# When eight DRAM to DRAM additions of a two-layer block are put into the DMA queue: two moved up, two moved behind a product

## The chip, the cores and the metric

The kernel runs on one core of one Trainium2 chip. The metric is the time of one launch on the device, in microseconds (us), as the median of several runs.

The engines are named as in the profile: PE multiplies matrices, ACT copies, casts and applies functions, DVE adds and subtracts, POOL and SP issue DMA transfers (POOL the adding ones, SP plain ones). Each engine takes its instructions in the order of the program and waits on semaphores.

## The reference

Attention with a sigmoid, a gated block, and a second block on the Fourier transform of the result. The change lies in the last product of the last block:

```python
X = np.fft.fft(x, axis=1)
X = np.fft.fft(X, axis=2)
mixed = np.real(X).astype(np.float32)
u = x + mixed
...
un = (u - mu) / np.sqrt(var + 1e-06)
ch = np.maximum(un @ w_ch1, 0.0) @ w_ch2
return (u + ch).astype(np.float32)
```

There are four batch rows of 448 tokens, 768 features, and 3072 hidden features. All is float32.

## The kernel before, in words

Batch rows 0 and 1 go through both products directly. Batch rows 2 and 3 go through them together, by a scheme with seven block products in the place of eight. The hidden features are taken in twelve groups `g` of 256. A first product (`pair1`, PE tiles `f_X`, `f_Y`, `f_Z`, `f_W`) makes two groups, and then a *pass* `p` of the second product (`second`, PE tiles `m_...`) takes these two groups. There are five passes, p = 0 to 4 (`NS` is 5); the last two groups go through the plain product at the end (PE `f<-extra,v_h` and `f<-h,v_h`), whose pieces DVE adds to `acc`.

One pass has seven products, k = 0 to 6, and each product has three pieces, e = 0 to 2. A piece is six matmuls of 128x448. PE leaves a piece in one of five PSUM banks (`bank2`), ACT copies it into one of six slots of the tile `stage` (`second_done`, line 1204), and POOL adds the slot to a sum in DRAM by a DMA with `accum_op=add` (line 244), or to two sums. So a slot is free again when its additions have landed, and a bank when ACT has copied it. A piece that ACT can't copy for want of a slot holds the bank; five pieces later PE waits.

The sums in DRAM are `u_d[2]` and `u_d[3]` (six tiles each, one for each 128 features; `first(b)` is tiles 0 to 2, `last(b)` tiles 3 to 5) and four helpers `m_d[0]` to `m_d[3]` of three tiles each. Which product goes where is written in `second_done`. In the passes before the last, products 0 to 3 go to `m_d[0]` to `m_d[3]`, product 4 to `first(2)`, product 5 to `last(2)`, product 6 to `first(3)`. In the last pass product 0 goes to `m_d[3]` and `first(2)` at once, product 1 to `last(3)` and `first(3)` at once: two additions for each piece.

The generator `combine` adds the helpers into the sums where they belong, by DMAs from DRAM to DRAM of 672 KB (or 448 and 224 KB): `m_d[0]` into `m_d[3]` and `first(2)`, `m_d[1]` into `last(3)` and `first(3)`, `m_d[3]` into `m_d[2]` and `first(3)`, and at the end `m_d[2]` into `last(2)` and `last(3)`. Then it loads `u_d[2]` and `u_d[3]` into `acc`, in four loads on SP, for the additions of the plain product.

The order of instructions comes from a clock of the planner (`Order`): each generator yields the planned time at which it wants to go on, `need` waits for a key's planned time, and what a generator calls is put on its engine's queue at that point. On the chip the order of each queue is then fixed, and the waits are semaphores. Two DMAs on the same bytes wait for each other's landing, and a DMA that waits holds up all that stands behind it on POOL.

In the program's rows `u_d_141` is `u_d[2]`, `u_d_142` is `u_d[3]`, and `m_d_219` to `m_d_222` are `m_d[0]` to `m_d[3]`.

Of the kernel before, what the change touches and what calls it, by code (L numbers as in the profile page):

```python
# [111 lines left out]
NS = NG // 2 - 1  # L112
# [140 lines left out]
def build(tc, ap):  # L253
    nc = tc.nc
    V, G = nc.vector, nc.gpsimd
    o = Order(nc)
# [945 lines left out]
    def second_done(p, k, e, ps):  # L1202
        st = m_t["stage"][:, (3 * (7 * p + k) + e) % KD]
        yield o.act(st, ps)
        if k > 3:
            outs = [u_d[2 + k // 6][:, e + 3 * (k == 5)]]
        elif p < NS - 1 or k > 1:
            outs = [m_d[k][:, e]]
        elif k == 0:
            outs = [m_d[3][:, e], u_d[2][:, e]]  # L1210
        else:
            outs = [u_d[3][:, e + 3], u_d[3][:, e]]
        t = max([o.dma(out, st, add=p > 0 or k > 3) for out in outs])
        o.at["sum", k, e, p] = t + 6.0
        yield o.now

    def combine():

        def first(b):
            return u_d[b][:, 0:3]  # L1220

        def last(b):
            return u_d[b][:, 3:6]

        def landed(*ks, p=NS - 1):
            yield from o.need(*(("sum", k, e, p) for k in ks for e in range(3)))

        yield from landed(0, 3, p=NS - 2)
        for c in (slice(0, 2), slice(2, 3)):
            o.dma(m_d[3][:, c], m_d[0][:, c], add=True)  # L1230
        yield o.now + 8.0
        o.dma(first(2), m_d[0], add=True)
        yield from landed(6, p=NS - 2)
        o.dma(last(3), m_d[1], add=True)
        yield o.now + 8.0
        o.dma(first(3), m_d[1], add=True)
        yield from landed(0, 2, 3)
        for c in (slice(0, 2), slice(2, 3)):
            o.dma(m_d[2][:, c], m_d[3][:, c], add=True)
        o.dma(first(3), m_d[3], add=True)  # L1240
        yield o.now + 10.0
        o.dma(last(2), m_d[2], add=True)
        o.dma(last(3), m_d[2], add=True)
        yield from o.need(("hs", 7 * NS - 1))
        acc[2] = np_.tile([128, KD, S], F32, tag="x2", name="acc2", bufs=3)
        t = o.dma(acc[2][:, 0:3], first(2)) + 4.0
        o.at.update((("accs", 2, e), t) for e in range(3))
        yield from landed(5)
        t = o.dma(acc[2][:, 3:6], last(2)) + 4.0
        o.at.update((("accs", 2, e), t) for e in range(3, 6))  # L1250
        yield from landed(6)
        acc[3] = np_.tile([128, KD, S], F32, tag="x2", name="acc3", bufs=3)
        for x, src, es in ((acc[3][:, 0:3], first(3), range(3)), (acc[3][:, 3:6], last(3), range(3, 6))):
            t = o.dma(x, src) + 4.0
            o.at.update((("accs", 3, e), t) for e in es)
        yield o.now
# [71 lines left out]
    def network():  # L1328
# [88 lines left out]
        def second(p, ks):  # L1417
            for k in ks:
                m = 7 * p + k
                yield from o.need(("sw", m), ("hs", m))  # L1420
                (wh, wl), hs = sw_t[m], hs_t[m]
                for e in range(3):
                    es = slice(128 * e, 128 * e + 128)

                    def pair(i, wh=wh, wl=wl, hs=hs, es=es):
                        return wh[:, i, es], wl[:, i, es], hs[i][:, 0], hs[i][:, 1]

                    mark = ("part", m, e)
                    yield from o.tile(partial(bank2, f"m_{m}_{e}"), 2, pair, partial(second_done, p, k, e), mark)
                while len(o.feed) > 6:  # L1430
                    yield o.now + 0.1
            while ("part", m, 2, 1) not in o.at:
                yield o.now + 0.1
# [57 lines left out]
    o.spawn(late_rows())  # L1491
    o.spawn(second_rows())
    o.spawn(combine())
    o.spawn(second_weights())
    o.spawn(second_weights2())
# [64 lines left out]
```

## Time and profile before

| | |
|---|---|
| median of three runs | 1195.19 us (1195.03 to 1195.59) |
| time of the profiled execution | 1194.45 us |
| its span | 1192.7 us |
| PE busy | 1175.1 us, 99% of the span |
| DVE, ACT, POOL busy | 890.8, 575.0, 101.7 us |
| bytes in HBM | 149.35 MB read, 103.86 MB written |

The span is that of the engines' instructions, and the time of the execution has 1.75 us around it. A busy PE is one with a matmul in it, at whatever clock: the granted clock of TensorE is 1 at 2.4 GHz and 0.5 at 1.2 GHz.

### The profile page before, as it was taken

To read this page: it belongs to the slowest core of one execution; us is meant where nothing else is said; L and a number is where in the kernel's file an instruction comes from. 1 tells how busy PE (TensorE), PEld (TensorE's weight loads), DVE (VectorE), ACT (ScalarE), POOL (GpSimd) and SP (SyncE) were. 2 spreads that over 40 slices of the span, in tenths; PEclk is the share of its full clock that TensorE was granted. 3 is DMA by queue.
4 is the path that set the end of the run, shared out by engine and by line. 5 is a ranking of instruction groups with operands and counts; after the bars stand their busy time and mean duration, and the time that the engine had idled before them with its cause. 6 is when DMAs were issued, how large, how long until landed. Compare 5 with 4: busy or idle time off the path is not lost.

```text
span 1192.7 us, 16593 instructions
## 1 busy us (share of the span) xinstructions
PE 1175.1 (99%) x6040; PEld 1028.7 (86%) x6040; DVE 890.8 (75%) x1442; ACT 575.0 (48%) x1054; POOL 101.7 (9%) x142
## 2 busy tenths in 40 slices
PE   8999999999999999999999999999999999999798
PEld 3477767789999999999999999999999999999698
DVE  5686897656853669797999989899577777777472
ACT  5877777757540122242333333333247667665440
POOL 0000000000000000000000000000000234243530
PEclk9999999999999999999999999999999999999899
DMA  6757679766948556386556555645917598889996
GB/s 221 223 177 243 238 233 351 250 237 231 321 170 257 194 166 220 101 311 236 184 195 212 205 205 190 240 173 186 348 65 221 92 189 133 172 177 194 206 169 208
DMA packets 95009, 248.79 MB, mean 209 GB/s; under 512 B 11280, under 2 KB 48208, under 8 KB 94544
## 3 DMA queue, kind: packets, MB, share of 16 engines
q1 hardware_dynamic: 78416, 216.90, 52.5%
q0 software_dynamic: 16368, 30.62, 15.7%
q8 instruction: 47, 0.77, 0.3%
q14 instruction: 34, 0.28, 0.1%
q10 hardware_dynamic: 144, 0.23, 0.1%
HBM read 149.35 MB, written 103.86 MB: 212 GB/s over the span
## 4 chain that ended last, share of the span: by engine, by line
PE 92%; DMA 4%; DVE 2%; ACT 1%; issue 0%; POOL 0%; SPq 0%; ACTq 0%; DVEq 0%; POOLq 0%
PE f L185 31%; PE k L185 10%; PE v L185 9%; PE m L185 7%; PE r L185 7%; PE av L185 6%; PE sc L185 6%; PE f_W L185 3%; PE f_Z L185 3%; PE f_X L185 3%; PE f_Y L185 2%; PE pq L185 1%; DMA k<-k_d 1%; DMA w<-w_d 1%; DMA u_d<-m_d 1%; PE pa L185 1%
## 5 line engine op out<-in xcount | busy, mean ns | idle before, releaser
L185 PE MATMUL f<-un,w1h 128*128 128x448 f32 x576 | 163.7, 364 | 0.0
L185 PE MATMUL f<-h,w2h 128*128 128x448 f32 x576 | 162.8, 363 | 0.0
L228 DVE SCALAR_TENSOR_TENSOR w_bits<-w_raw,w_bits 128x768 uint32<-128x768 uint32 (+1 forms) x120 | 114.5, 954 | 1.7
L185 PEld LDWEIGHTS f<-un,w1h 128*128 128x128 f32 x576 | 108.1, 188 | 7.3 <-issue 0.4
L185 PEld LDWEIGHTS f<-h,w2h 128*128 128x128 f32 x576 | 108.0, 188 | 7.3 <-DVE acc L220 0.3
L185 PE MATMUL v<-k,wvh 128*128 128x448 f32 x384 | 112.4, 366 | 0.4 <-DMA k<-k_d 0.4
L239 ACT ACTIVATE sg<-sc,bias_s 128x448 f32<-128x448 f32 x168 | 94.8, 647 | 20.8 <-PE sc L185 20.8
L244 POOL DMA_DIRECT2D u_d<-stage x54 | 50.6, 1080 | 630.8 <-ACT stage L237 612.4
L185 PE MATMUL f<-un,w1l 128*128 128x448 f32 x288 | 104.0, 361 | 0.0
L185 PE MATMUL f<-h,w2l 128*128 128x448 f32 x288 | 103.8, 361 | 0.0
L220 DVE TENSOR_TENSOR acc<-acc,f 128x448 f32<-128x448 f32 x126 | 76.3, 617 | 35.0 <-PE f L185 27.7
L185 PE MATMUL m<-hs,sw_h 128*128 128x448 f32 x324 | 92.7, 366 | 8.4 <-ACT stage L237 8.2
L185 PE MATMUL av<-sg,v 128*64 128x448 f32 (+1 forms) x336 | 82.4, 550 | 0.2 <-ACT sg L239 0.2
L185 PEld LDWEIGHTS v<-k,wvh 128*128 128x128 f32 x384 | 71.6, 188 | 6.7 <-DMA k<-k_d 1.8
L185 PEld LDWEIGHTS m<-hs,sw_h 128*128 128x128 f32 x324 | 61.2, 189 | 13.1 <-ACT stage L237 8.6
L185 PE MATMUL v<-k,wvl 128*128 128x448 f32 x192 | 70.3, 366 | 0.0
L185 PE MATMUL k<-xkh,wkh 128*128 128x448 f32 x192 | 70.0, 365 | 0.0
L185 PE MATMUL k<-xkh,wkl 128*128 128x448 f32 x192 | 69.6, 362 | 0.0
L185 PE MATMUL k<-xkl,wkh 128*128 128x448 f32 x192 | 69.5, 362 | 0.0
L237 ACT COPY stage<-m 128x448 f32<-128x448 f32 x105 | 55.3, 536 | 28.3 <-DMA u_d<-stage 14.5
L185 PEld LDWEIGHTS av<-sg,v 128*64 128x64 f32 (+1 forms) x336 | 27.7, 143 | 44.1 <-issue 30.0
L239 ACT ACTIVATE w_raw<-w_raw 128x768 f32<-128x768 f32 x40 | 36.7, 918 | 58.7 <-DVE w_bits L228 45.6
(216 smaller groups left out, 2587.3 us busy)
## 6 DMA issues: line engine op xcount, KB each, us to landing
w_raw<-in_w SPq DMA_DIRECT2D x40, 768.0 KB, 4.7
w_d<-w_bits SPq DMA_DIRECT2D x40, 384.0 KB, 2.6
k_d<-kp SPq DMA_DIRECT2D x32, 448.0 KB, 3.1
k<-k_d SPq DMA_DIRECT2D x32, 448.0 KB, 6.4
u_d<-stage POOLq DMA_DIRECT2D x54, 224.0 KB, 6.1
m_d<-stage POOLq DMA_DIRECT2D x45, 224.0 KB, 6.6
a<-w_d SPq DMA_DIRECT2D x24, 384.0 KB, 3.9
w<-w_d SPq DMA_DIRECT2D x24, 384.0 KB, 7.4
```

The lines of the kernel that those rows point to most:

```text
L185: self.nc.tensor.matmul(out, lhs, rhs, start=start, stop=stop, skip_group_check=skip)
L220: eng.tensor_tensor(out, a, c, op=op)
L228: self.nc.vector.scalar_tensor_tensor(out, a, scalar, c, op0=op0, op1=op1)
L237: self.nc.scalar.copy(out, a)
L239: self.nc.scalar.activation(out, a, fn, **kw)
L244: self.nc.gpsimd.dma_start(out, src, accum_op=ALU.add)
```

## The change

`second_done` notes when the additions of a piece were put into the queue (`added`). In `combine`, the addition of `m_d[1]` into `last(3)` no longer waits for product 6 of the last pass but one: it goes right behind the addition of `m_d[0]` into `first(2)`. The addition of `m_d[1]` into `first(3)` goes in as soon as product 6 of that pass is in the queue, and not 8 planned us after the one into `last(3)`. The last two, of `m_d[2]` into `last(2)` and `last(3)`, are put behind product 5 of the last pass.

```diff
@@ second_done
         t = max([o.dma(out, st, add=p > 0 or k > 3) for out in outs])
         o.at["sum", k, e, p] = t + 6.0
+        o.at["added", k, e, p] = o.now
         yield o.now
@@ combine
         yield o.now + 8.0
         o.dma(first(2), m_d[0], add=True)
-        yield from landed(6, p=NS - 2)
         o.dma(last(3), m_d[1], add=True)
-        yield o.now + 8.0
+        yield from o.need(("added", 6, 2, NS - 2))
         o.dma(first(3), m_d[1], add=True)
         yield from landed(0, 2, 3)
         for c in (slice(0, 2), slice(2, 3)):
             o.dma(m_d[2][:, c], m_d[3][:, c], add=True)
         o.dma(first(3), m_d[3], add=True)
-        yield o.now + 10.0
+        yield o.now + 8.0
+        yield from o.need(("added", 5, 2, NS - 1))
         o.dma(last(2), m_d[2], add=True)
         o.dma(last(3), m_d[2], add=True)
```

POOL's queue from the additions of products 5 and 6 of pass 3 to product 1 of pass 4, with the semaphores that each row waits for. Before:

```order
L244 DMA u_d_142<-stage 128x448 [waits Activation_49] x2
L244 DMA u_d_142<-stage 128x448 [waits DMASW7_49,Activation_49]
L244 DMA u_d_142<-m_d_220 128x1344 [waits DMASW0_49]
L244 DMA m_d_222<-stage 128x448 [waits DMASW1_49,Activation_49]
L244 DMA u_d_141<-stage 128x448 [waits DMASW2_49]
L244 DMA m_d_222<-stage 128x448 [waits DMASW3_49,Activation_49]
L244 DMA u_d_141<-stage 128x448 [waits DMASW4_49]
L244 DMA m_d_222<-stage 128x448 [waits DMASW5_49,Activation_49]
L244 DMA u_d_141<-stage 128x448 [waits DMASW6_49]
L244 DMA u_d_142<-m_d_220 128x1344 [waits DMASW7_49]
L244 DMA u_d_142<-stage 128x448 [waits DMASW0_49,Activation_49]
L244 DMA u_d_142<-stage 128x448 [waits DMASW7_49,DMASW1_49]
```

The same place in the changed kernel:

```order
L244 DMA u_d_141<-m_d_219 128x1344 [waits DMASW6_49,DMASW5_49,DMASW4_49]
L244 DMA u_d_142<-m_d_220 128x1344
L244 DMA u_d_141<-stage 128x448 [waits Activation_49] x3
L244 DMA u_d_142<-stage 128x448 [waits Activation_49]
L244 DMA u_d_142<-stage 128x448 [waits DMASW7_49,Activation_49]
L244 DMA u_d_142<-stage 128x448 [waits DMASW0_49,Activation_49]
L244 DMA u_d_142<-m_d_220 128x1344 [waits DMASW6_49,DMASW7_49,DMASW1_49,DMASW0_49]
L244 DMA m_d_222<-stage 128x448 [waits DMASW2_49,Activation_49]
L244 DMA u_d_141<-stage 128x448 [waits DMASW3_49]
L244 DMA m_d_222<-stage 128x448 [waits DMASW4_49,Activation_49]
L244 DMA u_d_141<-stage 128x448 [waits DMASW5_49]
L244 DMA m_d_222<-stage 128x448 [waits Activation_49]
```

The first 672 KB addition of `m_d_220` has moved ahead of the six additions of products 5 and 6; the second, which stood between product 0's and product 1's additions, now stands ahead of product 0's, and waits for the three of product 6 just ahead of it to land.

POOL's queue at its end, from product 5 of pass 4 on. Before, with the 672 KB addition of `m_d_222` ahead:

```order
L244 DMA u_d_142<-m_d_222 128x1344
L244 DMA u_d_141<-stage 128x448 [waits Activation_49]
L244 DMA u_d_141<-stage 128x448 [waits DMASW4_49,Activation_49]
L244 DMA u_d_142<-stage 128x448 [waits DMASW5_49,DMASW2_49,Activation_49]
L244 DMA u_d_142<-stage 128x448 [waits DMASW6_49,Activation_49]
L244 DMA u_d_142<-stage 128x448 [waits DMASW7_49,Activation_49]
L244 DMA u_d_141<-m_d_221 128x1344 [waits DMASW3_49,DMASW4_49,DMASW1_49,DMASW0_49]
L244 DMA u_d_142<-m_d_221 128x1344
```

The same place in the changed kernel:

```order
L244 DMA u_d_142<-m_d_222 128x1344
L244 DMA u_d_141<-stage 128x448 [waits Activation_49] x2
L244 DMA u_d_141<-stage 128x448 [waits DMASW4_49,Activation_49]
L244 DMA u_d_141<-m_d_221 128x1344 [waits DMASW4_49,DMASW5_49,DMASW3_49,DMASW7_49,DMASW2_49,DMASW0_49]
L244 DMA u_d_142<-m_d_221 128x1344 [waits DMASW6_49]
L244 DMA u_d_142<-stage 128x448 [waits DMASW1_49,Activation_49]
L244 DMA u_d_142<-stage 128x448 [waits Activation_49] x2
```

The two additions of `m_d_221` have moved ahead of product 6's three, and wait for product 5's three to land.

ACT's queue in pass 4, from the casts for product 4 (`hs`) to the third copy of product 3. The planner's clock for DMAs has shifted, and with it rows that the diff doesn't name. Before:

```order
L237 COPY stage<-m_2_10803 128x448
L237 CAST hs_0_10817<-rows 128x448
L237 CAST hs_1_10818<-rows 128x448
L237 CAST sw_h<-w_4_10371 128x768
L237 COPY stage<-m_0_10821 128x448
L237 CAST blk_10785<-a_0_10685 128x384
L237 COPY stage<-m_1_10833 128x448
L237 COPY stage<-m_2_10843 128x448
```

The same place in the changed kernel, up to the second copy of product 3:

```order
L237 CAST hs_0_10807<-rows 128x448
L237 CAST hs_1_10808<-rows 128x448
L237 COPY stage<-m_1_10793 128x448
L237 CAST blk_10759<-a_0_10686 128x384
L237 COPY stage<-m_2_10805 128x448
L237 COPY stage<-m_0_10820 128x448
L237 CAST sw_h<-w_4_10371 128x768
L237 COPY stage<-m_1_10832 128x448
```

The cast `sw_h`, the last that reads the weights `w_4`, has moved behind the copy of product 3's first piece; SP's loads of the next weights wait for it. The casts for product 4 and one of `blk` have moved ahead of that copy.

## Rows read from the trace of the kernel before

**Rows 1.** The page's first part: busy us, share, instructions.

```profile
PE 1175.1 (99%) x6040; PEld 1028.7 (86%) x6040; DVE 890.8 (75%) x1442; ACT 575.0 (48%) x1054; POOL 101.7 (9%) x142
```

**Rows 2.** PE's timeline in pass 4: start us, us, instruction, count, [idle before].

```profile
1115.06 0.37 PE L185 MATMUL m<-hs,sw_l 128*128 128x448 f32 x1
1123.62 1.11 PE L185 MATMUL m<-hs,sw_h 128*128 128x448 f32 x2 [8.19 <-ACT stage L237]
...
1126.03 3.36 PE L185 MATMUL f_X<-B,blk 128*128 128x448 f32 x9
1129.23 1.97 PE L185 MATMUL f_Y<-T,blk 128*128 128x448 f32 x9
1131.03 1.96 PE L185 MATMUL f_Z<-T,blk 128*128 128x448 f32 x9
```

**Rows 3.** Stretches: length, busy us of PE, PEld, DVE, ACT, POOL; clock, DMA, GB/s.

```profile
1115.00:1124.00 9.00, 0.81 (x4) 0.43 (x3) 0.41 (x1) 0.94 (x2) 7.14 (x9) 0.71 0.99 243
1124.00:1130.00 6.00, 6.00 (x19) 5.33 (x19) 1.72 (x3) 2.85 (x7) 2.55 (x4) 0.58 1.14 203
```

**Rows 4.** The chain that ended last, in this stretch: start us, us, what.

```profile
1104.64 9.98 DMA u_d<-m_d
...
1115.13 7.81 DMA u_d<-stage
```

**Rows 5.** ACT's timeline in pass 4.

```profile
1111.22 0.54 ACT L237 COPY stage<-m 128x448 f32<-128x448 f32 x1 [1.71 <-DMA u_d<-stage]
...
1112.58 0.83 ACT L237 CAST sw_h<-w 128x768 fp32r<-128x768 f32 x1
1123.04 0.53 ACT L237 COPY stage<-m 128x448 f32<-128x448 f32 x1 [9.62 <-DMA u_d<-stage]
```

**Rows 6.** POOL's timeline: the issue of additions.

```profile
1078.41 0.81 POOL L244 DMA_DIRECT2D u_d<-m_d  x1 [5.49 <-DMA u_d<-stage]
...
1087.83 1.18 POOL L244 DMA_DIRECT2D u_d<-m_d  x1
1100.27 0.87 POOL L244 DMA_DIRECT2D m_d<-stage  x1 [11.26 <-ACT stage L237]
...
1104.64 1.76 POOL L244 DMA_DIRECT2D u_d<-m_d  x1
...
1115.13 4.37 POOL L244 DMA_DIRECT2D u_d<-stage  x5 [7.83 <-DMA u_d<-m_d]
...
1159.03 2.03 POOL L244 DMA_DIRECT2D u_d<-m_d  x2
```

**Rows 7.** DMA from issue to landing, one each: issued 1078.41, 1087.83, 1100.27, 1145.19.

```profile
u_d<-m_d POOLq DMA_DIRECT2D x1, 672.0 KB, 7.1
...
u_d<-m_d POOLq DMA_DIRECT2D x1, 672.0 KB, 10.6
...
m_d<-stage POOLq DMA_DIRECT2D x1, 224.0 KB, 4.0
...
u_d<-stage POOLq DMA_DIRECT2D x1, 224.0 KB, 13.3
```

**Rows 8.** DMA queues, 1123 to 1131 us, POOL's (q0): packets, MB, share.

```profile
q0 software_dynamic: 1015, 1.62, 114.4%
```

**Rows 9.** The same, 1066 to 1076 us: POOL's queue and SP's (q1).

```profile
q0 software_dynamic: 703, 1.15, 63.9%
q1 hardware_dynamic: 597, 1.64, 45.2%
```

**Rows 10.** SP's timeline in pass 4.

```profile
1114.43 1.75 SPq L246 DMA_DIRECT2D w<-w_d  x4
```

**Rows 11.** DVE's timeline in pair1 behind pass 4's product 4.

```profile
1133.31 0.55 DVE L220 TENSOR_TENSOR blk<-a,blk 128x384 fp32r<-128x384 f32 x1
1133.78 0.62 DVE L220 TENSOR_TENSOR u<-u,f_Z 128x448 f32<-128x448 f32 x1
```

**Rows 12.** DVE's timeline in the plain product at the end.

```profile
1162.44 0.62 DVE L220 TENSOR_TENSOR acc<-acc,f 128x448 f32<-128x448 f32 x1 [0.51 <-PE f L185]
1164.84 0.62 DVE L220 TENSOR_TENSOR acc<-acc,f 128x448 f32<-128x448 f32 x1 [1.78 <-PE f L185]
...
1174.56 1.69 DVE L220 TENSOR_TENSOR acc<-acc,f 128x448 f32<-128x448 f32 x3 [6.70 <-DMA acc<-u_d]
```

## The prediction

> **What bounds the kernel now.** The page's first part comes first: PE holds a matmul for 1175.1 of 1192.7 us [rows 1], so the kernel is bound by PE, and only time in which PE stands still or runs at the lower clock can be won. PE's timeline shows where that is. In pass 4, between the second and the third piece of product 4, PE stands for 8.19 us, until 1123.62, for a copy into `stage` [rows 2]. By the page PE is idle for 17.6 us in all, so this is nearly half of it.
>
> The stall has a second price. The granted clock, 1 before, has a mean of 0.71 in the stretch of the stall and of 0.58 in the next 6 us [rows 3], so PE fell to 1.2 GHz during the stall. Nine matmuls of `f_Y` take 1131.03 - 1129.23 = 1.80 us, 0.20 each. The six of the piece behind the stall take 1126.03 - 1123.62 = 2.41 us in the place of 1.20, and the nine of `f_X` 3.20 in the place of 1.80 [rows 2]. That is 2.61 us. Stall and clock together cost 8.19 + 2.61 = **10.8 us**.
>
> Why did ACT not copy? The chain names the cause: a 672 KB addition issued at 1104.64 lands after 9.98 us, at 1114.62; only then is an addition issued, at 1115.13, and it lands after 7.81, at 1122.94; ACT's copy starts at 1123.04, having waited 9.62 [rows 4, 5]. POOL shows the same as a gap of 7.83 us ahead of the addition at 1115.13 [rows 6]. The large one is `m_d[1]` into `first(3)`. Behind it in the queue stands product 1's addition into the same tiles, which has to wait for its landing, and so holds up all additions behind it, those that free the slots among them.
>
> **The change part by part.** No transfer is added or removed; eight change their place.
>
> *The addition into `last(3)`*, before at 1087.83, goes right behind that into `first(2)`, which is issued at 1078.41 and lands 7.1 us later, at 1085.5 [rows 6, 7]. What does POOL's queue take for one? Full, it moves 1.62 MB in 8 us, 203 GB/s [rows 8]: 1.13 us for 224 KB, 3.4 for 672 KB. The moved one lands at about 1088.9, the six additions of products 5 and 6 by 1088.9 + 6.8 = 1095.7. They free slots that are wanted from about 1099.5 on, as the first addition of pass 4 is issued at 1100.27 [rows 6]. So this costs nothing, with some 4 us of cover.
>
> *The addition into `first(3)`* waits for product 6's landings and is issued 0.5 us later (as 1115.13 follows 1114.62), at about 1096.2. POOL has nothing else until 1100.27, so this new wait is covered too. From issue to landing I take the 7.1 of rows 7 (the other, 10.6, stood behind six additions); it lands at 1103.3, and product 1's addition into `first(3)`, issued near 1105, finds it done. The 7.83 us gap goes. This is the change's gain.
>
> *What is late next: the additions themselves.* Products 0 and 1 make two additions a piece, twelve in 7.2 us of PE (six pieces of 1.20), and the queue needs 12 x 1.13 = 13.6. The last slot of product 0 came free near 1111.1, as ACT's copy at 1111.22 had waited for a landing [rows 5]; the queue ahead is empty then as now, since the first addition takes 4.0 us to land, until 1104.3 [rows 7]. So I keep 1111.1. Product 1's six follow, the second at 1113.4, the last at 1117.9. The second frees the slot for product 3's first piece, whose copy ends at 1113.9; PE wants its bank at 1123.62 - 8.19 = 1115.43. No stall there, with 1.5 us in hand.
>
> The next ones are tighter. The cast `sw_h` now stands behind that copy, so it starts at 1113.9, and SP's four weight loads, which came 1.85 us after its start before (1112.58 to 1114.43, [rows 5, 10]), start at about 1115.8. Beside such loads POOL's queue moved 1.15 MB in 10 us [rows 9], 1.99 us for 224 KB. So product 2's additions land at 1119.9, 1121.9 and 1123.9. The last of them frees the slot for product 4's third piece; right behind its copy ACT copies `f_X` out of its bank, at 0.54 us each until 1125.0. Without a stall PE wants to use that bank again at 1115.43 + 1.20 + 4 x 1.80 = 1123.83: **1.2 us** of stall. Then ACT casts a block (0.5 like its copies), and DVE works it off in its order: `blk`, `u`, `a`, `u`, 0.55 + 0.62 + 0.55 + 0.62 [rows 11], with the cast 2.85, until 1127.85; the next product wants the second `u` at 1125.0 + 1.8 = 1126.8: **1.05 us** more. Together 2.3 us of new waits.
>
> Bounds: if the weight loads cost the queue nothing (1.13 for each addition), the last slot is free at 1121.3, the casts ahead on ACT let the copy of `f_X` end at 1123.3, and 0.5 us stay. If the addition into `first(3)` takes 10.6, it lands at 1106.8, the twelve behind it come 2.5 us later, PE waits 1.1 for the bank and is held by as much more as the queue is late: 4.8 us. I take 2.3, the row beside weight loads being the nearest.
>
> The Trainium skill (DMA: Bandwidth & Descriptors, "Anatomy of one DMA — SWDGE (gpsimd) path") gives a fixed 2.0 us and then 436 GB/s for a DMA of this queue, about 0.5 us of moving for 224 KB. The trace disagrees: 1.13 with the queue full [rows 8]. By the Trainium skill the additions would never be late, the new waits would be none, and the sum would be that of the first rival below.
>
> *The last two additions* now wait for product 5's landings and stand ahead of product 6's three. Before, product 5's last landed 13.3 us after its issue at 1145.19 [rows 7], at 1158.5, behind the additions from the helpers; the two themselves were issued at 1159.03 [rows 6]. So even at the old pace they start no later, and product 6's three land some 2 x 3.4 us later than they would ahead of them. What waits is the plain product: DVE's fourth addition waited 6.70 us for a load already [rows 12], and PE did not stand, as it can run five banks (five pieces of 2.40 us, the spacing in rows 12) ahead. That cover of 12 us hides it. I take nothing for this part.
>
> **Sum.** 10.8 - 2.3 = 8.5 us less: 1194.45 - 8.5 = 1185.95 for the profiled execution, which lies 0.74 below the median of the runs, so **1186.7** on that scale. With the bounds, 10.3 and 6.0 us less: 1184.9 to 1189.2.
>
> **Rivals.**
> - *Nothing is left of the stall.* The additions land as fast as the slots are asked for. For it: DVE and PE have no other wait of weight. Against: 13.6 us of queue in 7.2 us of PE. 1195.19 - 10.8 = 1184.4.
> - *The short waits bring the low clock back.* For it: the one long stall did. Against: PE is busy between the two, and no row shows what a wait of 1 or 2 us does. The low stretch before cost 2.61 us with half of it idle; twice that behind busy matmuls, 5.1, gives about 1191.8.
> - *The stall stays whole.* It is not the wait for the landing but the twelve additions that fill the slots. The row for it is ACT's wait at 1111.22, which comes before the gap. It decides if product 1's second addition lands not at 1113.4 but near 1122.9 as before; that takes a further 9.5 us in the queue. About 1195.2, no change.
> - *Slower: the end.* Product 6's three additions, behind two of 672 KB, come so late that the loads into `acc` outlast the five banks. Rows 12 speak for it, as a load is late there already. By my sum the two land near 1158 and 1161 and product 6's by 1165 (all 8.5 earlier than at the old pace, 7.1 and 3.4 apart), the load of `first(3)` some 5 later, at 1170. The seventh piece, the first that needs it, ends at 1162.44 + 6 x 2.40 - 8.5 = 1168.3, and PE would stand for its bank four pieces later, from 1178 on. Each us beyond that is a us lost, and it passes the gain only if the load comes at 1187. At 3 us worse than before: 1198.
>
> **How the numbers follow.** A measurement can tell 0.2%, 2.4 us. Chances: forecast 0.64 (1184.9 to 1189.2), nothing left 0.10, low clock 0.10, stall whole 0.10, slower 0.06. The first three are all faster than 1192.8: 0.84 faster, 0.10 same, 0.06 slower. The range runs from 1184.0, a little under the first rival, to 1192.2, just past the second, and leaves out the last two, 0.16, and what stands close to its ends.
>
> **What would show it.** In the changed profile PE should have no idle time near 1115 us and no gap on POOL ahead of product 1's additions; the large addition into `first(3)` should be issued near 1096 and land near 1103; the weight loads should start near 1116; PE should wait for ACT's copy of `f_X` and for DVE's `u` near 1124 to 1128, 2.3 us together, at a clock of 1. The loads into `acc` should find PE still running. The prediction is wrong if PE stands for a `stage` copy again, if the clock falls, or if PE waits in the plain product.

## The result: 1185.84 us, and the profile after

The changed kernel takes 1185.84 us (median of five runs, 1185.33 to 1187.09). The kernel before, run beside it, takes 1195.59 us (five runs, 1195.03 to 1196.62). The ratio is 0.9919, with a 95% interval of 0.9905 to 0.9934, which is 7.9 to 11.4 us less. 1186.7 was forecast.

The profiled execution took 1185.84 us, with a span of 1184.1 us, so it is 8.6 us shorter than the one before. By the page's first part PE is busy for 1171.7 us, 3.4 less than in [rows 1]; 2.6 of that is what the prediction counts for the stretch at 1.2 GHz.

PE's timeline in pass 4, in the columns of [rows 2]:

```profile
1114.23 0.36 PE L185 MATMUL m<-hs,sw_l 128*128 128x448 f32 x1
1115.39 0.67 PE L185 MATMUL m<-hs,sw_h 128*128 128x448 f32 x2 [0.80 <-ACT stage L237]
...
1118.51 1.96 PE L185 MATMUL f_Y<-T,blk 128*128 128x448 f32 x9
...
1125.12 2.08 PE L185 MATMUL f_X<-B,blk 128*128 128x448 f32 x9 [1.05 <-ACT u L237]
1127.75 2.05 PE L185 MATMUL f_Z<-T,blk 128*128 128x448 f32 x9 [0.55 <-ACT blk L237]
```

The stall of 8.19 us has become one of 0.80. Two new ones stand where they were forecast, 1.05 and 0.55 us. At the first `f_Y` PE is 1129.23 - 1118.51 = 10.72 us ahead of before, and at the `f_Z` behind the new waits still 8.68 (before it began at 1131.03 + 3 x 1.80 = 1136.43, [rows 2]). From there on the lead stays near 8.6. It is not all the change's: PE was 0.83 us ahead at the piece in front of the stall already (1114.23 against 1115.06). Nor does that lead come from the change. At an `f_X` of an earlier first product, where the order of every queue is still the same in both, the profile of the changed kernel is 1.56 us ahead already; here the row of before and that of the changed kernel:

```profile
1065.15 1.97 PE L185 MATMUL f_X<-B,blk 128*128 128x448 f32 x9
```

```profile
1063.59 1.97 PE L185 MATMUL f_X<-B,blk 128*128 128x448 f32 x9
```

About 1 us of this is lost again in two waits of PE for `blk`, 0.62 us at 1086.38 and 0.33 at 1088.79, which neither the profile before nor a second profile of the changed kernel (`changed_again`, below) has. So the 8.6 us of these two spans hold some chance, and the gain goes by the runs' times.

The windows of three stretches, with the columns of [rows 3], give a granted clock of 1 throughout:

```profile
1113.00:1118.00 5.00, 4.20 (x21) 3.50 (x20) 0.96 (x1) 2.27 (x5) 2.63 (x4) 1.00 1.14 202
...
1124.00:1130.00 6.00, 4.40 (x21) 3.76 (x21) 4.99 (x10) 3.86 (x8) 1.70 (x2) 1.00 1.12 266
```

POOL's timeline, as [rows 6]:

```profile
1095.74 0.83 POOL L244 DMA_DIRECT2D u_d<-m_d  x1 [8.03 <-DMA u_d<-stage]
1099.85 0.87 POOL L244 DMA_DIRECT2D m_d<-stage  x1 [3.27 <-ACT stage L237]
...
1104.09 4.71 POOL L244 DMA_DIRECT2D u_d<-stage  x5
...
1147.96 1.69 POOL L244 DMA_DIRECT2D u_d<-m_d  x2 [9.25 <-DMA u_d<-stage]
```

The addition into `first(3)` is issued at 1095.74, behind a wait of 8.03 us in which POOL has nothing to issue that anyone wants yet. Product 1's additions are among the five that start at 1104.09, with no gap ahead, where 7.83 us stood before.

### The profile page after: what moved, and what is told of

Its sections match the earlier page's. It is cut to its first block, busy times and chain, and to the rows that moved or that the text cites. A ratio compares the mean times of both kernels' runs of the same rounds, so it can differ in the third digit from the quotient of the medians.

```text
span 1184.1 us, 16590 instructions
## 1 busy us (share of the span) xinstructions
PE 1171.7 (99%) x6040; PEld 1026.3 (87%) x6040; DVE 890.6 (75%) x1442; ACT 574.3 (49%) x1054; POOL 101.0 (9%) x142
## 4 chain that ended last, share of the span: by engine, by line
PE 93%; DMA 3%; DVE 2%; ACT 1%; POOL 0%; issue 0%; SPq 0%; ACTq 0%; DVEq 0%
PE f L185 32%; PE k L185 10%; PE v L185 9%; PE m L185 7%; PE r L185 7%; PE av L185 6%; PE sc L185 6%; PE f_Z L185 3%; PE f_W L185 3%; PE f_X L185 3%; PE f_Y L185 2%; PE pq L185 1%; DMA w<-w_d 1%; DMA u_d<-stage 1%; PE pa L185 1%; PE qa L185 1%
```

## Experiments

**Theory:** the stall came from one thing, the place of the 672 KB addition into `first(3)` between product 0's and product 1's additions; the two other moves carry nothing. **Rivals:** the addition into `last(3)`, moved up, thins out the queue and has part in the gain; the last two, moved behind product 5, cost or give something at the end; or it is the order of ACT's and DVE's queues in pass 4, which the planner shifted along with the transfers. A second question is what the 2.4 us that are left come from: weight loads that slow the queue, as the prediction had it, or something else. In the diffs `-` is the changed kernel (in the second experiment the kernel before).

**1. Only the transfer into `first(3)` late again** (`first3_late`).

```diff
-        yield from o.need(("added", 6, 2, NS - 2))
+        yield from o.need(("added", 0, 2, NS - 1))
         o.dma(first(3), m_d[1], add=True)
```

> The changed kernel with one addition put back: m_d[1] into first(3) stands between product 0's and product 1's additions of the last pass again; the one into last(3) stays early. Theory: the addition behind it waits for its landing, POOL has its gap of 6 to 8 us, PE stands 6 to 8 us and the clock falls: 1193 to 1197. Rival (what mattered was the addition into last(3), or the number of additions): 1185 to 1188.

It took 1195.55 us (11 runs, 1193.58 to 1197.37) beside 1195.37 before: ratio 1.0001 (0.9992 to 1.001). The whole gain is gone. POOL's and PE's timelines and the windows show it:

```profile
1107.65 1.51 POOL L244 DMA_DIRECT2D u_d<-m_d  x1
...
1118.62 4.38 POOL L244 DMA_DIRECT2D u_d<-stage  x5 [8.56 <-DMA u_d<-m_d]
```

```profile
1123.31 1.12 PE L185 MATMUL m<-hs,sw_h 128*128 128x448 f32 x2 [5.75 <-ACT stage L237]
1135.18 2.08 PE L185 MATMUL f_X<-B,blk 128*128 128x448 f32 x9 [1.48 <-ACT u L237]
1137.81 2.05 PE L185 MATMUL f_Z<-T,blk 128*128 128x448 f32 x9 [0.54 <-ACT blk L237]
```

```profile
1120.00:1127.00 7.00, 3.69 (x10) 3.32 (x11) 0.96 (x1) 2.21 (x4) 6.67 (x9) 0.51 1.10 164
```

The gap on POOL, a `stage` copy that comes late for PE and the low clock come back together, with `last(3)` and the last two in their new places. The stall is shorter than before, 5.75 us and not 8.19, and the short waits for `f_X` and `f_Z`, 2.02 us, come on top. The last of the rivals is settled here too: ACT and DVE go through pass 4 in the changed kernel's order, past the stall and the short waits, and only POOL's order differs. ACT's timeline has `sw_h` behind the copy, as in the changed kernel:

```profile
1122.72 0.53 ACT L237 COPY stage<-m 128x448 f32<-128x448 f32 x1 [8.07 <-DMA u_d<-stage]
1123.15 0.83 ACT L237 CAST sw_h<-w 128x768 fp32r<-128x768 f32 x1
```

**2. Only the last two moved** (`last_two_alone`), from the kernel before, with the key `added` put in as in the change:

```diff
-        yield o.now + 10.0
+        yield from o.need(("added", 5, 2, NS - 1))
         o.dma(last(2), m_d[2], add=True)
         o.dma(last(3), m_d[2], add=True)
```

> The kernel before with only the two additions of m_d[2] moved ahead of product 6's three. Theory: 1194 to 1197, ratio to before 0.999 to 1.001, with the stall of about 8 us and the low clock in place. Rival (the two last additions carry part of the gain): 1189 to 1193, ratio below 0.998.

1195.63 us (11 runs) beside 1195.37: ratio 1.0001 (0.9993 to 1.001). The stall stands as before, and the clock behind it is low:

```profile
1126.56 1.12 PE L185 MATMUL m<-hs,sw_h 128*128 128x448 f32 x2 [8.48 <-ACT stage L237]
```

```profile
1127.00:1134.00 7.00, 7.00 (x29) 6.36 (x29) 2.57 (x5) 4.17 (x10) 3.75 (x5) 0.78 1.14 203
```

**3. All but the last two moved** (`m1_alone`): the pair of `m_d[2]` stands behind product 6 again.

```diff
-        yield o.now + 8.0
-        yield from o.need(("added", 5, 2, NS - 1))
+        yield from o.need(("added", 6, 2, NS - 1))
         o.dma(last(2), m_d[2], add=True)
```

> Only the two additions of m_d[1] are moved; the two of m_d[2] stand behind product 6 of the last pass, as before the change. Theory (the gain is that no addition waits any more for the 672 KB into first(3) between products 0 and 1): 1185 to 1187, the changed kernel's time, ratio to before 0.991 to 0.993; PE does not wait in the plain product. Rival (the two last additions carry part of the gain, because they free the queue's end): 1188 to 1192.

1186.55 us (1185.60 to 1187.98), ratio 0.9927 (0.9915 to 0.9939): within its interval the gain of the whole change. So the last two neither give nor cost what can be measured, in either company.

**4. `last(3)` left in its old place** (`last3_old_place`, and `last3_again` in another comparison):

```diff
         o.dma(first(2), m_d[0], add=True)
-        o.dma(last(3), m_d[1], add=True)
         yield from o.need(("added", 6, 2, NS - 2))
+        o.dma(last(3), m_d[1], add=True)
         o.dma(first(3), m_d[1], add=True)
```

> The changed kernel with the addition of m_d[1] into last(3) behind product 6 of the last pass but one again, where it stood before the change, and the one into first(3) right behind it, still ahead of product 0. Theory (only the place of the one into first(3) counts; product 6's additions land some 2 us earlier when last(3) is not ahead of them, so that into first(3) lands by 1102 and not at 1104.8): at most the changed kernel's time, 1183.5 to 1186, with 0.5 to 2 us of the 2.4 us of waits. Rival (moving last(3) up is part of the gain): 1187 or more.

> The changed kernel with the addition into last(3) back behind product 6 of its own pass. Theory (that addition has room in either place and carries nothing): 1184.5 to 1186, at most 1.5 us below the changed kernel, and the transfer into first(3) lands sooner since less stands ahead of it. Rival (moving last(3) up is part of the gain): 1.5 us or more above the changed kernel.

1185.49 us, ratio 0.9909 (0.9896 to 0.9923), and 1185.02, ratio 0.9913 (0.9900 to 0.9927). Moving `last(3)` up has no part in the gain. In the first of the two profiled executions PE's wait for the bank was gone and that for `f_X` was 0.45 us:

```profile
1123.12 2.07 PE L185 MATMUL f_X<-B,blk 128*128 128x448 f32 x9 [0.45 <-ACT u L237]
```

In the second they were 0.58 and 0.88 us. So that it is faster than the change is not shown: the changed kernel, timed once more beside the second, took 1185.69.

> The changed kernel once more, as the measure for the two beside it: 1185 to 1187 us, three waits of TensorE of 0.5 to 1.1 us at the place of the change.

Its ratio was 0.9917 (0.9903 to 0.9930), which holds that of the variant. Its profile has the three waits again, of 0.71, 1.05 and 0.54 us.

**5. Only `first(3)` moved** (`first3_alone`): both edits of 3 and 4 together, so that against the kernel before one addition of the eight has changed its place (and, by the planner, the order of ACT and DVE in pass 4, which gains nothing without it by experiment 1).

> Of the whole change only the addition of m_d[1] into first(3) is moved up; last(3) stays behind product 6 of its pass, and the last pair into the plain product's sums stays ahead of the last product as before. Theory (this one transfer holds the whole of the stall): 1184.5 to 1186.5 us, no low clock. Rival (the three moves share the gain): 1188 us or more.

1186.15 us, ratio 0.9922 (0.9908 to 0.9935), against 0.9917 for the whole change on the same chip. One transfer is the whole of it. In its profiled execution PE waited 0.65 us for `f_X`, 0.55 for `f_Z` and 0.58 for a later `blk`, none for the bank.

**6. The weight loads held back** (`w_held`) until product 6 of pass 4 is planned:

```diff
+            if p == NS:
+                yield from o.need(("prod", 14 * NS + 6))
             w = ws2.tile([128, 2, 2, D], F32, tag="w2", name=f"w2_{p}", bufs=1)
```

> The changed kernel with SP's four weight loads of 1.5 MB for the plain product held back until the first product of group 10 is done, some 13 us later. Theory (beside these loads the queue's additions take 2.2 in the place of 1.1 us, and that makes PE wait for the copy of f_X and for the sum u): these two waits, 1.05 and 0.55 us, shrink to 0.5 together, the wait for a bank ahead of them, 0.80, stays; 1184 to 1185.5. Rival (the twelve additions alone make them): the waits stay, 1185.8. Either is spoiled if the weights come too late for the plain product: PE would stand there.

1189.10 us, ratio 0.9950 (0.9937 to 0.9964): slower than the change, where 1184 to 1185.5 was expected. That the loads slow the queue is confirmed. Without them the additions of product 2, issued at 1113.25, 1114.36 and 1115.49, land 8.5 us later each and so 1.1 us apart to the last; in the changed kernel the spacing grows to 2.2 (below).

```profile
m_d<-stage POOLq DMA_DIRECT2D x3, 224.0 KB, 8.5
```

PE's timeline:

```profile
1125.80 2.08 PE L185 MATMUL f_X<-B,blk 128*128 128x448 f32 x9 [0.30 <-ACT u L237]
1128.42 2.05 PE L185 MATMUL f_Z<-T,blk 128*128 128x448 f32 x9 [0.54 <-ACT blk L237]
1139.12 0.67 PE L185 MATMUL m<-hs,sw_h 128*128 128x448 f32 x2 [0.82 <-ACT stage L237]
```

The wait for `f_X` falls from 1.05 to 0.30 us. How much of this is the loads' is not shown: the wait for the bank, which was expected to stay, is gone in this profile too, and with the loads in their place that for `f_X` is 0.40 to 0.65 us in the three profiles that have it and no wait for the bank (`first3_after_m3`, `last3_old_place`, `first3_alone`). That for `f_Z` is 0.54 to 0.56 in every profile here that has one for `f_X`, of whatever size (0.30 to 1.48), and absent where that one is: its size is not the queue's. Later the loads meet those of `a`, ACT waits 5.76 us for one, and PE for 0.82 and 0.27:

```profile
1138.12 0.51 ACT L237 CAST blk<-a 128x384 fp32r<-128x384 f32 x1 [5.76 <-DMA a<-w_d]
```

But these four waits are 1.93 us, less than the 2.40 of the change, and where the rest of the 1189.10 us comes from stays open. By the profiles 2.95 us are there long before the loads, at the `f_X` that begins at 1063.59 in the changed kernel, where the order of every queue is the same in both:

```profile
1066.54 1.97 PE L185 MATMUL f_X<-B,blk 128*128 128x448 f32 x9
```

**7. `first(3)` moved the other way** (`first3_after_m3`), behind the addition of `m_d[3]`:

```diff
-        yield from o.need(("added", 6, 2, NS - 2))
-        o.dma(first(3), m_d[1], add=True)
...
         o.dma(first(3), m_d[3], add=True)
+        o.dma(first(3), m_d[1], add=True)
```

> The changed kernel with the addition of m_d[1] into first(3) put behind that of m_d[3] into first(3), so that nothing of 672 KB stands near products 0 and 1. Theory (the 2.4 us left are due to twelve additions that start 1.3 us late behind it): the waits shrink to 0.5 to 1.5, and the end has room for 3.4 us more of queue: 1183.5 to 1185.5. Rival (the end has no room): PE stands in the plain product, 1186 to 1190.

1188.07 us, ratio 0.9931 (0.9918 to 0.9945). The stall in pass 4 is gone here too, but the end has no room for it. POOL's, DVE's and PE's timelines:

```profile
1143.62 0.81 POOL L244 DMA_DIRECT2D u_d<-m_d  x1 [13.22 <-DMA u_d<-m_d]
...
1154.39 1.69 POOL L244 DMA_DIRECT2D u_d<-m_d  x2 [7.30 <-issue]
```

```profile
1169.78 1.69 DVE L220 TENSOR_TENSOR acc<-acc,f 128x448 f32<-128x448 f32 x3 [11.90 <-DMA acc<-u_d]
```

```profile
1170.45 0.68 PE L185 MATMUL f<-h,v_h 128*128 128x448 f32 x2 [1.23 <-DVE acc L220]
```

The second addition into `first(3)` waits 13.22 us for the first to land, and holds up the queue behind it. The last pair is issued 6.4 us later than in the changed kernel, DVE waits 11.90 us for a load into `acc`, and PE stands for 1.23 us in the plain product; from its last matmul's start to the end of the span it takes 5.9 us and not 4.2. This is the mechanism of the prediction's slower rival, set off by another order.

**8. Product 1 added once** (`m1_once`): in the last pass it goes to `m_d[1]` alone, so that products 0 and 1 make nine additions and not twelve, and `m_d[1]` goes into both sums behind `m_d[3]`.

```diff
-        elif p < NS - 1 or k > 1:
+        elif p < NS - 1 or k > 0:
             outs = [m_d[k][:, e]]
...
-        o.dma(last(3), m_d[1], add=True)
-        yield from o.need(("added", 6, 2, NS - 2))
-        o.dma(first(3), m_d[1], add=True)
...
         o.dma(first(3), m_d[3], add=True)
+        o.dma(first(3), m_d[1], add=True)
+        o.dma(last(3), m_d[1], add=True)
```

> Product 1 of the last pass is added into m_d[1] as in the other passes, three additions in the place of six, and m_d[1] goes into first(3) and last(3) behind m_d[3]: nine additions for products 0 and 1 in the place of twelve. Theory (the queue's twelve additions in 7.2 us make what is left of the stall): all three waits go (below 0.6 together), 1182.5 to 1184.5, and the end holds 6.8 us more of queue within the five banks. Rival (the end has no room): the loads into acc come too late, PE stands in the plain product, 1186 to 1190.

1187.05 us, ratio 0.9928 (0.9915 to 0.9942). All three short waits of pass 4 are gone, but PE's timeline shows two others in the next pair of groups, for `blk`:

```profile
1137.88 2.30 PE L185 MATMUL f_X<-B,blk 128*128 128x448 f32 x9 [1.57 <-ACT blk L237]
1141.20 2.27 PE L185 MATMUL f_Y<-T,blk 128*128 128x448 f32 x9 [1.03 <-ACT blk L237]
```

Why `blk` comes late there stays open; 2.60 us of waits in the place of 2.40 leave nothing won. The time lies in the range of the expectation's rival, but not by its mechanism: PE does not stand in the plain product. No variant is measurably faster than the change.

## Why the prediction was right

**The cause of the stall.** Right, and shown: experiment 1 brings a stall and the whole time back with this transfer alone, and experiment 5 takes the whole gain with it alone. Of the eight additions the edit moves four, not eight as the prediction has it, and one of these counts. No run separates the low clock from the stall: where the stall of 5.75 us or more was, the clock fell, and where it was not, it stayed.

**The moved additions and the new wait of POOL.** Right. Product 6's additions had landed by 1095.74 (forecast 1095.7), and the addition into `first(3)` was issued then (1096.2). Experiment 4 bears out "this costs nothing" for `last(3)`, which also means that its move was of no use.

**"7.1 from issue to landing" and "the queue ahead is empty".** The first is a size that varies, the second is wrong. DMA issues, KB each and median us from issue to landing, of the stretch at 1095.5 and of that at 1099.7 in the changed kernel:

```profile
u_d<-m_d POOLq DMA_DIRECT2D x1, 672.0 KB, 9.0
a<-w_d SPq DMA_DIRECT2D x1, 384.0 KB, 2.9
...
m_d<-stage POOLq DMA_DIRECT2D x1, 224.0 KB, 5.9
```

With loads of `a` beside it, it took 9.0 us and landed at 1104.8, between the forecast 1103.3 and the upper bound of 1106.8. In the second profile of the same kernel (`changed_again`), at 1094.9 and 1099.5, it took 7.4 and landed at 1102.3, ahead of the forecast, and PE waited for the bank all the same:

```profile
u_d<-m_d POOLq DMA_DIRECT2D x1, 672.0 KB, 7.4
...
m_d<-stage POOLq DMA_DIRECT2D x1, 224.0 KB, 4.8
```

```profile
1114.96 0.68 PE L185 MATMUL m<-hs,sw_h 128*128 128x448 f32 x2 [0.71 <-ACT stage L237]
```

So 9.0 in the place of 7.1 is not what makes the wait. In both, product 0's first addition is issued (1099.85 and 1099.53) while the large one is still on its way, and takes 5.9 and 4.8 us, not 4.0 [rows 7]. With no large one ahead of it (`first3_after_m3`) it takes 3.9, and PE has no wait for the bank. By the prediction's own numbers the queue was not empty: a transfer that lands at 1103.3 is still on its way at 1100.27. The seven profiles that have it in this place point the same way: where it landed up to 1.6 us behind the issue of product 0's first addition there is no wait for the bank (`last3_old_place`, `first3_alone`), where it was 2.8 us or more the wait is 0.53 to 0.80, and at 2.1 it is none in one (`w_held`) and 0.58 in the other (`last3_again`).

In the changed kernel the twelve additions started late, and all behind them came 1.3 us later than forecast. The chain shows product 1's second addition landing at 1105.17 + 9.54 = 1114.71, where 1113.4 was forecast:

```profile
1105.17 9.54 DMA u_d<-stage
```

PE wanted the bank at 1114.59, 0.84 us before the forecast time. The 1.5 us in hand were gone by these two, and 0.80 us of wait came that only the upper bound had.

**The additions beside the weight loads.** Right in the end, by luck: two errors of 1.3 and 1.2 us cancel, a late start, and loads that slow the queue later than forecast. ACT's `sw_h` started at 1115.23 and SP's loads at 1117.09, each 1.3 us after its forecast time, by the same shift of the queue:

```profile
1115.23 0.84 ACT L237 CAST sw_h<-w 128x768 fp32r<-128x768 f32 x1
```

```profile
1117.09 1.89 SPq L246 DMA_DIRECT2D w<-w_d  x4
```

The three additions of product 2 and the next, issued at 1111.81, 1112.94, 1114.07 and 1115.63, landed 8.5, 8.8, 9.9 and 10.5 us later:

```profile
m_d<-stage POOLq DMA_DIRECT2D x1, 224.0 KB, 8.5
m_d<-stage POOLq DMA_DIRECT2D x1, 224.0 KB, 8.8
m_d<-stage POOLq DMA_DIRECT2D x1, 224.0 KB, 9.9
m_d<-stage POOLq DMA_DIRECT2D x1, 224.0 KB, 10.5
```

That is at 1120.3, 1121.8, 1124.0 and 1126.1. The first is still spaced like those of a queue that works alone; 2 us and more apart they are only from the third on, as the loads, issued from 1117.09 on, come to move. So the last of product 2 landed at 1124.0, where 1123.9 was forecast. DMA queues of the changed kernel, from 1106 to 1117 us and from 1121 to 1130, in the columns of [rows 8]:

```profile
q0 software_dynamic: 1376, 2.19, 113.5%
...
q0 software_dynamic: 673, 1.07, 66.3%
```

2.19 MB in 11 us are 1.15 us for 224 KB, as in [rows 8]; 1.07 MB in 9 us are 1.93, as in [rows 9] (1.99). By the rate of the Trainium skill that the prediction weighed (DMA: Bandwidth & Descriptors, "Anatomy of one DMA — SWDGE (gpsimd) path"), an estimate of about 0.5 us for each, the additions would not have been late. The trace disagrees again, with 1.15 and 1.93.

**The waits for `f_X` and `f_Z`.** Right in place, and nearly in size. ACT's and DVE's timelines:

```profile
1124.10 0.53 ACT L237 COPY stage<-m 128x448 f32<-128x448 f32 x1 [0.34 <-PE f_W L185]
1124.53 0.54 ACT L237 COPY u<-f_X 128x448 f32<-128x448 f32 x1
...
1127.10 0.51 ACT L237 CAST blk<-a 128x384 fp32r<-128x384 f32 x1 [1.62 <-DVE a L220]
```

```profile
1125.51 0.56 DVE L220 TENSOR_TENSOR blk<-a,blk 128x384 fp32r<-128x384 f32 x1 [0.97 <-ACT blk L237]
1125.99 0.61 DVE L220 TENSOR_TENSOR u<-u,f_Y 128x448 f32<-128x448 f32 x1
1126.52 0.55 DVE L220 TENSOR_TENSOR a<-a 128x384 f32<-128x384 f32 x1
1126.99 0.61 DVE L220 TENSOR_TENSOR u<-u,f_Z 128x448 f32<-128x448 f32 x1
```

The copy at 1124.10 is put down to PE's `f_W`, which fills no `m` bank; it follows the landing at 1124.0, and the landing is the likelier releaser. ACT's copy of `f_X` ended at 1125.07 (forecast 1125.0) and PE waited 1.05 us (1.2). DVE did its steps in the forecast order, and `f_Z` came free at 1127.75 (1127.85). By the profile PE waited there for ACT's cast of `blk` behind DVE's `a`, and not for the second `u`; the two end within 0.02 us of each other (1127.61 and 1127.60), so either would have held PE. The 0.55 us, where 1.05 was forecast, is in part a matter of counting: the profile's idle time begins when the last matmul's modelled end is past. By starts PE lost 1127.75 - (1125.12 + 9 x 0.20) = 0.83 us.

**The last two.** Right: issued at 1147.96, not later than before, and in DVE's timeline a load into `acc` is waited for 4.04 us, in the place of the 6.70 of [rows 12], with no wait of PE behind it:

```profile
1163.30 1.15 DVE L220 TENSOR_TENSOR acc<-acc,f 128x448 f32<-128x448 f32 x2 [4.04 <-DMA acc<-u_d]
```

**The sum.** 0.80 + 1.05 + 0.55 = 2.40 us of new waits by the profile's count, where 2.3 was forecast. That they agree so well is luck. The forecast counts by starts, and by starts the three are 0.96 + 1.21 + 0.83 = 3.0 us. The first of them was taken at nothing, with 1.5 us in hand; the two others were forecast at 2.25 and came to 2.04. All lies within the bounds of 0.5 to 4.8.

The rivals: the time alone does not tell the forecast from the first one (nothing left of the stall, 1184.4), as the interval of the gain, 7.9 to 11.4 us, holds both 8.5 and 10.8; the waits in the profiles do. The clock was 1 behind waits of this size; the stall did not stay; the end had room. Two slips change nothing: twice 2.61 is 5.2 and not 5.1, and the lower bound's 0.5 us is given without its working.

## What to carry to other kernels

A DMA that adds to bytes which another addition is still writing waits in this program for its landing, and on POOL's queue everything behind it waits too (7.83 us before, 13.22 in experiment 7). In a kernel like this one look for the large transfer that stands between two uses of the same bytes, and move it to where the queue is idle ahead of the burst; of this change that one line was worth all, and the lines beside it nothing that could be measured. And when a stall of 8 us is taken away, the next work that was just in time behind it comes short by 2 us: follow each slot and each load that waited in the shadow of the stall before counting the gain.

## What the runs showed of the hardware

- The same 672 KB addition, with loads of `a` in flight, took 9.0 us from issue to landing in one profile of the changed kernel and 7.4 in the other, and 6.8 in `last3_old_place`; where it stood among 224 KB additions it took 10.0 [rows 4], 10.5 (`first3_late`) and 11.1 (`last_two_alone`).
- 224 KB additions from a full POOL queue came 1.1 us apart, and 1.9 to 2.2 beside SP's loads.
- The granted clock stayed at 1 behind waits of PE of up to 1.57 us (`m1_once`, 1.00 from 1130 to 1145 us), and was 0.51 in the 7 us in and behind the wait of 5.75 (`first3_late`).
